# Moving the SBUF start addresses of weights, activations and gates in a fused attention and gated feed-forward kernel

## The chip, the cores and the metric

The kernel runs on one core of a Trainium2 chip. The metric is the device time of one execution in microseconds (us), the median of several runs. The text also speaks of the *span*: the time from the first to the last instruction of one profiled execution.

## The reference

Eight batches of eight attention heads: 512 local positions (which see 32 global keys and a band of local keys within 32 positions) and 32 global positions (which see all keys). The heads' outputs side by side form x, and a feed-forward block with a depthwise convolution as its gate follows.

```
s_g = scale * np.matmul(q_g, k_all.transpose(0, 1, 3, 2))
out_g = np.matmul(sm(s_g), v_all)
mask = np.abs(pos[:, None] - pos[None, :]) <= window          # window = 32
s_ll = np.where(mask, s_ll, -1000000000.0)
out_l = np.matmul(sm(np.concatenate([s_lg, s_ll], axis=-1)), np.concatenate([v_g, v_l], axis=2))
x = np.concatenate([out_g, out_l], axis=2)    # heads side by side: (8, 544, 512)
h = np.maximum(x @ w_in, 0.0)                 # (8, 544, 1024)
conv_out[:, s] = sum(conv_w[k] * h[:, s + k - 1] for k in range(3))
return (h * sigmoid(conv_out)) @ w_out        # (8, 544, 512)
```

## The kernel before

Everything lies with 128 rows in SBUF's 128 partitions. x, the gates g and both weight matrices are held as two float32r parts each, a high and a low one, and a product is the sum of three matmuls: high by high, high by low, low by high.

- **Attention** (lines 292 to 516): scores S (line 333) and G (line 354), maximum with mask (366), exponential (376), normalisation (390 or 397), 32x32 transposes (405), P·V (429). These are small matmuls that share the array in tiles of 32 or 64 rows.
- **x.** `XH` and `XL` (lines 447 and 455) write a batch's x, `[P, 2, NCT, SL]`: high and low part, four chunks of 512 columns of 2,048 bytes. The 32 global rows and the two rows beside them of all batches go to `xg` (line 271), `[P, 2, NCT, 8, 34]`, whose chunks are 272 columns, 1,088 bytes.
- **Up projection, `Z`** (line 533, matmul on 541): for each of 8 blocks of 128 hidden columns and each of 4 chunks three matmuls with a 128x128 block of `w_in` as weights. They come in runs of six (`Za`, `Zb`). A batch has 96 of 512 columns; the last unit, for the collected rows, has 96 of 272 columns that read `xg`.
- **Gate**: `RE` (ReLU into `hb`, one of two buffers that take turns from one pair of blocks to the next; line 554 on ScalarE), `C1` (317, GpSimd), `Ca` and `Cb` (568, VectorE), `TH` (575, ScalarE), `GG` (579, VectorE), `GH` and `GL` (278 and 281), which write g, `[P, 2, 2, SL]`.
- **Down projection, `O`** (line 591, matmul on 599): 4 blocks of output columns, 24 matmuls each, in runs of six (`Oa` to `Od`), weights from `w_out`. The last unit's have 278 columns. `OE` (line 278 again) and `ST` (611) store the result.
- **Weights** come as two 32-bit words per number in 8 pieces (`raw`, line 205, in the slots that g uses later), are taken apart on ScalarE, VectorE and GpSimd (`wt`, lines 141 to 163, in the slots of the gate's `t`), and for the first four pieces TensorE forms the low part in three matmuls per half (lines 257 to 259).

The order on every engine is fixed: `emit` (line 1038) plans all steps with a table of costs and due times and ties each instruction to the one ahead of it on its engine.

**SBUF addresses.** Tiles lie in the order in which pools are entered and tiles are made: `const` (line 89), `load`, `att`, `small` (92), `xp` (93, two slots of x), `moe` (94: `t` and `o`), `gp` (95: five slots of g). Every tile is rounded up to 32 bytes. `GM` (line 471) takes the negated maximum of a global softmax in a small tile of two columns, `GE` (482) takes the sum of the exponentials in another of one column, and `GN` and `GS` read that.

Of the kernel before, what the change touches and what calls it, by code (L numbers as in the profile page):

```python
# [11 lines left out]
F32 = mybir.dt.float32  # L12
# [6 lines left out]
P = 128  # L19
# [65 lines left out]
def attn_moe(ctx: ExitStack, tc: tile.TileContext, q_d, k_d, vw_d, qg_d, w_in_d, w_out_d, cw_d, out_d):  # L85
# [3 lines left out]
    const = ctx.enter_context(tc.tile_pool(name="const", bufs=1))  # L89
    load = ctx.enter_context(tc.tile_pool(name="load", bufs=2))  # L90
    att = ctx.enter_context(tc.tile_pool(name="att", bufs=2))
    small = ctx.enter_context(tc.tile_pool(name="small", bufs=4))
    xp = ctx.enter_context(tc.tile_pool(name="xp", bufs=SLOTS["x"]))
    moe = ctx.enter_context(tc.tile_pool(name="moe", bufs=2))
    gp = ctx.enter_context(tc.tile_pool(name="gp", bufs=SLOTS["g"]))
# [100 lines left out]
    def choice(key):  # L196
        return ENGS[phase[0]][key]

    w_in = [const.tile([P, NFT, NCT, P], F32R, name=f"w_in{i}") for i in range(2)]
    w_out = [const.tile([P, NCT, NFT, P], F32R, name=f"w_out{i}") for i in range(2)]  # L200
    raw = {}
# [269 lines left out]
    def GM(n):  # L471
        gr = groups[n]
        pg = gr["pg"] = pgs[n % 2]
        negm = gr["m"] = small.tile([P, 2], F32, name="gnegm", bufs=SLOTS["pg"])
        for i, (ps, sl) in enumerate(((gr["s0"], slice(SG, S)), (gr["s1"], slice(0, SG)))):
            nc.vector.tensor_scalar(  # L476
                out=pg[:, sl], in0=ps, scalar1=-SCALE, scalar2=None, op0=ALU.mult, op1=ALU.min,
                accum_out=negm[:, i : i + 1],
            )
        nc.vector.tensor_tensor(out=negm[:, 0:1], in0=negm[:, 0:1], in1=negm[:, 1:2], op=ALU.min)  # L480

    def GE(n):
        gr = groups[n]
        gr["r"] = small.tile([P, 1], F32, name="gsum", bufs=SLOTS["pg"])
        nc.scalar.activation(
            out=gr["pg"][:, 0:S], in_=gr["pg"][:, 0:S], func=AF.Exp, scale=-1.0, bias=gr["m"][:, 0:1], accum_out=gr["r"]
        )
# [120 lines left out]
    def ST(o):  # L608
# [5 lines left out]
        LQ=LQ, LK=LK, LV=LV, XC=XC, LG=LG, G=G, S=SC, M=MA, E=EX, NS=NS, NP=NP, DT=DT, P=PV,  # L614
        XH0=lambda n: XH(n, 0), XH1=lambda n: XH(n, 1), XL0=lambda n: XL(n, 0), XL1=lambda n: XL(n, 1),
        GM=GM, GE=GE, GN=GN, GX=GX, GS=GS, XG=XG,
        Za=lambda u: Z(u, 0), Zb=lambda u: Z(u, 1), RE=RE, C1=C1, Ca=lambda u: C2(u, 0), Cb=lambda u: C2(u, 2), TH=TH, GG=GG, GH=GH, GL=GL,
        Oa=lambda o: O(o, 0), Ob=lambda o: O(o, 1),
# [11 lines left out]
SLOTS = dict(  # L630
    ps=4, pa=2, x=2, hb=2, q=3, k0=1, k1=1, k2=1, k3=1, vf=2, qg=2, p0=2, p1=2, m=6, r=3, pg=2, go=2, t=2, o=2, g=5,
)
# [454 lines left out]
def program(arrays):  # L1087
    import concourse.bacc as bacc

    nc = bacc.Bacc("TRN2", target_bir_lowering=False, num_devices=1, dynamic_dma_scratch_size=1024)  # L1090
    args = [nc.dram_tensor(n, a.shape, mybir.dt.from_np(a.dtype), kind="ExternalInput").ap() for n, a in arrays.items()]
    args = [a.bitcast(U32) if a.dtype == mybir.dt.uint64 else a for a in args]
    B = arrays["q"].shape[0]
    out = nc.dram_tensor("out", (P, NCT * (B * (SL + GV) - 2)), F32, kind="ExternalOutput").ap()
    with tile.TileContext(nc, schedule_with_timeline_sim=True) as tc:
        attn_moe(tc, *args, out)
    return nc
# [19 lines left out]
```

## Time and profile before

| | |
|---|---|
| median of 3 runs | 543.51 us (543.3 to 543.71) |
| the profiled execution's own time | 543.3 us |
| its span | 541.4 us |
| TensorE matmul busy | 498.3 us (92%) of the span |
| VectorE, ScalarE, GpSimd busy | 420.5, 332.9, 102.9 us |
| matmuls of Z and O with 512 columns | 768 + 768 |
| matmuls of Z with 272 columns, of O with 278 | 96 + 96 |

PE is TensorE's matmul, PEld its weight load (which runs beside matmuls), DVE VectorE, ACT ScalarE, POOL GpSimd, SP the queue that issues DMAs. A matmul's duration in the rows includes its way through the array, so matmuls that follow each other overlap: their spacing is read from a run of several, or from the starts of two neighbours. An execution's time exceeds its span by 1.9 us here.

### The profile page before, as it was taken

What the parts mean: (1) busy time and instruction counts of PE and PEld (TensorE: products, weight loads), DVE (VectorE), ACT (ScalarE), POOL (GpSimd) and SP (SyncE); (2) the same over time, 40 slices, a digit from 0 to 9 for tenths busy, and PEclk for the clock granted to TensorE, in tenths of its full rate; (3) what the DMA queues carried; (4) which work ended last, traced back from release to release, by engine and by line L of the source; (5) the groups of instructions that cost most, each with busy time, mean ns of one, the idle gap of its engine ahead of it and who ended that gap; (6) DMA issues with size and microseconds to landing.
All of it is one profiled execution on the core that took longest, in us unless ns stands there. A gap on an engine that the chain in (4) does not pass through costs nothing.

```text
span 541.4 us, 16508 instructions
## 1 busy us (share of the span) xinstructions
PE 498.3 (92%) x6752; PEld 399.9 (74%) x6752; DVE 420.5 (78%) x1263; ACT 332.9 (61%) x1016; POOL 102.9 (19%) x153
## 2 busy tenths in 40 slices
PE   1945499989999999999999999999999999999997
PEld 0534378768788778788878877787878888888887
DVE  6988889999798878889788868987597884555451
ACT  3885969958658967983787239953379633233130
POOL 3474212442310111021011011111110211111110
PEclk9967689989999999999999999999999999999999
DMA  9986747341523231251324232410210000001101
GB/s 337 404 303 171 181 116 166 114 113 52 118 73 95 88 116 54 97 151 50 110 61 131 69 104 67 127 71 21 69 42 21 23 19 22 19 19 41 40 32 50
DMA packets 32668, 53.56 MB, mean 99 GB/s; under 512 B 2384, under 2 KB 20304, under 8 KB 31568
## 3 DMA queue, kind: packets, MB, share of 16 engines
q1 hardware_dynamic: 31440, 48.31, 26.8%
q0 software_dynamic: 1152, 4.19, 4.1%
q8 instruction: 53, 0.87, 0.7%
q14 instruction: 23, 0.19, 0.1%
HBM read 39.35 MB, written 8.96 MB: 89 GB/s over the span
## 4 chain that ended last, share of the span: by engine, by line
PE 88%; DVE 8%; ACT 2%; issue 1%; DMA 1%; SPq 0%; DVEq 0%
PE ps_o L599 36%; PE ps_h L541 35%; PE four L429 9%; PE four L333 5%; PE four L354 1%; ACT pt L376 1%; DVE pt L405 1%; DVE wt L154 1%; DVE t L568 1%; DVE pt L366 1%; DMA cwr<-cw 1%; PE psw L257 1%; DVE x L457 1%; DVE pg L476 1%; DVE wt L151 0%
## 5 line engine op out<-in xcount | busy, mean ns | idle before, releaser
L599 PE MATMUL ps_o<-g,w_out 128*128 128x512 f32 (+1 forms) x864 | 211.5, 385 | 0.0
L541 PE MATMUL ps_h<-x,w_in 128*128 128x512 f32 x768 | 202.3, 401 | 5.9 <-DVE x L457 4.1
L599 PEld LDWEIGHTS ps_o<-g,w_out 128*128 128x128 f32 x864 | 154.9, 188 | 34.9 <-issue 1.7
L541 PEld LDWEIGHTS ps_h<-x,w_in 128*128 128x128 f32 x768 | 143.1, 189 | 42.0 <-DVE x L457 4.8
L568 DVE SCALAR_TENSOR_TENSOR t<-hb,cw,t 128x512 f32<-128x512 f32 (+1 forms) x144 | 103.2, 736 | 34.6 <-POOL t L317 34.0
L317 POOL TENSOR_SCALAR t<-hb,cw 128x512 f32<-128x512 f32 (+1 forms) x72 | 53.7, 750 | 325.8 <-ACT hb L554 279.3
L376 ACT ACTIVATE pt<-pt,negm 128x128 f32<-128x128 f32 x256 | 99.2, 394 | 12.5 <-DVE negm L366 12.5
L554 ACT ACTIVATE hb<-ps_h 128x512 f32<-128x512 f32 (+1 forms) x72 | 41.4, 575 | 84.7 <-PE ps_h L541 84.4
L390 ACT ACTIVATE pt<-pt,sums 128x128 f32<-128x128 f32 x224 | 69.0, 396 | 0.9 <-DVE sums L383 0.9
L575 ACT ACTIVATE t<-t 128x1024 f32<-128x1024 f32 (+1 forms) x36 | 36.6, 1016 | 37.4 <-DVE t L568 37.4
L429 PE MATMUL four<-pt,vf 32*64 32x128 f32 (+3 forms) x2560 | 48.9, 294 | 10.6 <-DVE pt L405 3.8
L429 PEld LDWEIGHTS four<-pt,vf 32*64 32x64 f32 x2560 | 44.5, 139 | 17.3 <-issue 9.3
L366 DVE CUSTOM_DVE_ANT_0 pt<-four,mask 128x128 f32<-128x128 f32 x256 | 55.6, 285 | 2.1 <-PE four L333 2.1
L405 DVE STREAM_TRANSPOSE pt<-pt 128x608 f32<-128x608 f32 (+1 forms) x64 | 52.2, 851 | 1.6 <-ACT pt L390 1.6
L579 DVE SCALAR_TENSOR_TENSOR t<-t,hb 128x1024 f32<-128x1024 f32 (+1 forms) x36 | 42.3, 1174 | 13.1 <-ACT t L575 12.8
L376 ACT ACTIVATION_READ_ACCUMULATOR pt<-pt,negm 128x1 f32 x256 | 49.5, 193 | 0.0
L278 ACT CAST g<-t 128x1024 fp32r<-128x1024 f32 (+1 forms) x36 | 36.2, 1005 | 14.9 <-DVE t L579 10.6
L281 DVE TENSOR_TENSOR g<-t,g 128x1024 fp32r<-128x1024 f32 (+1 forms) x32 | 37.8, 1182 | 7.0 <-ACT g L278 6.7
L333 PE MATMUL four<-k,q 64*32 64x128 f32 x2048 | 36.0, 288 | 6.9 <-DVE pg L476 3.6
L333 PEld LDWEIGHTS four<-k,q 64*32 64x32 f32 x2048 | 31.0, 111 | 13.6 <-issue 4.8
L278 ACT CAST x<-four 128x384 fp32r<-128x384 f32 x64 | 19.4, 383 | 22.5 <-PE four L429 19.6
L278 DVE COPY o<-ps_o 128x512 f32<-128x512 f32 (+1 forms) x28 | 18.3, 653 | 16.2 <-PE ps_o L599 16.2
(70 smaller groups left out, 329.7 us busy)
## 6 DMA issues: line engine op xcount, KB each, us to landing
vf<-vw SPq DMA_DIRECT2D x16, 640.0 KB, 4.6
q<-q SPq DMA_DIRECT2D x32, 256.0 KB, 4.0
out<-o SPq DMA_DIRECT2D x32, 256.0 KB, 2.1
k<-k SPq DMA_DIRECT2D x24, 320.0 KB, 3.7
raw<-w_in SPq DMA_DIRECT2D x4, 1024.0 KB, 8.3
raw<-w_out SPq DMA_DIRECT2D x4, 1024.0 KB, 12.3
k<-k SPq DMA_DIRECT2D x8, 448.0 KB, 3.5
wt<-raw POOLq DMA_DIRECT2D x4, 512.0 KB, 5.2
```

Source lines behind the costliest of these rows:

```text
L278: nc.scalar.copy(out=out, in_=in_) if choice(key) == "a" else eng(key).tensor_copy(out=out, in_=in_)
L317: nc.gpsimd.tensor_scalar(out=out, in0=in_, scalar1=by, scalar2=0.0, op0=ALU.mult, op1=ALU.add)
L333: nc.tensor.matmul(heads[n + j]["s"][c * SG : (c + 1) * SG, r, :], lhsT=q[rows, c, r * SG : (r + 1) * SG], rhs=keys[rows, c, a : a + P], s ...
L366: nc.vector.tensor_tensor_reduce(out=out, in0=st["s"][:, r, :], in1=mask[:, v : v + 4].rearrange("p a c -> p (a c)"), op0=ALU.add, op1=ALU ...
L376: nc.scalar.activation(out=p, in_=p, func=AF.Exp, scale=-1.0, bias=st["m"][:, r : r + 1], accum_out=two["r"][:, n % 2, r : r + 1],)
L390: nc.scalar.activation(out=p, in_=p, func=AF.Copy, scale=by[:, r : r + 1])
L405: nc.vector.transpose(out=t, in_=t)
L429: nc.tensor.matmul(out, lhsT=vf[rows, j, s, :], rhs=pt, start=s == order[0], stop=s == order[-1])
L541: nc.tensor.matmul(hid[u]["z"], lhsT=w[:, ft, ct, :], rhs=x, start=ct + i == 0, stop=ct == NCT - 1 and i == 2)
L568: nc.vector.scalar_tensor_tensor(out=t, in0=rows_of(u, k)[:, u % 2], scalar=cw[:, 3 * ft + k : 3 * ft + k + 1], in1=t, op0=ALU.mult, op1=A ...
L579: nc.vector.scalar_tensor_tensor(out=t, in0=t, scalar=1.0, in1=rows_of(u, 1), op0=ALU.add, op1=ALU.mult)
L599: nc.tensor.matmul(ps, lhsT=w_out[w][:, mt, ft, :], rhs=g[:, k, ft % 2, :], start=ft + i == 0, stop=ft == NFT - 1 and i == 2,)
```

## The change

Two tiles that nothing reads or writes are put in, one of 96 bytes between the pools `small` and `xp`, one of 128 bytes ahead of `w_in`. The sum of the global softmax moves into a third column of the tile of the maximum, so that one small tile per slot is left instead of two.

```
+    gap = ctx.enter_context(tc.tile_pool(name="gap", bufs=1))
+    gap.tile([P, 24], F32, name="gap")
     xp = ctx.enter_context(tc.tile_pool(name="xp", bufs=SLOTS["x"]))
...
+    const.tile([P, 32], F32, name="gap")
     w_in = [const.tile([P, NFT, NCT, P], F32R, name=f"w_in{i}") for i in range(2)]
...
-        negm = gr["m"] = small.tile([P, 2], F32, name="gnegm", bufs=SLOTS["pg"])
+        negm = gr["m"] = small.tile([P, 3], F32, name="gnegm", bufs=SLOTS["pg"])
...
-        gr["r"] = small.tile([P, 1], F32, name="gsum", bufs=SLOTS["pg"])
+        gr["r"] = gr["m"][:, 2:3]
```

The start addresses in the two built programs (bytes within a partition; "rest" is the remainder by 256):

| tile | start before | rest | start after | rest |
|---|---|---|---|---|
| `plus`, `minus`, `pg`, `pt`, `mask`, `k`, `cw` | | | the same | the same |
| `w_in`, two parts | 41600, 57984 | 128 | 41728, 58112 | 0 |
| `w_out`, two parts | 74368, 90752 | 128 | 74496, 90880 | 0 |
| `xg` | 107136 | 128 | 107264 | 0 |
| `hb`, two slots | 115840, 119968 | 128, 160 | 115968, 120096 | 0, 32 |
| `qg`, `vf`, `q` | from 124096 | 192 | from 124224 | 64 |
| `x`, two slots | 142944, 159328 | 96 | 143104, 159488 | 0 |
| `t` and `wt`, two slots | 175712, 179808 | 96 | 175872, 179968 | 0 |
| `o`, two slots | 183904, 185952 | 96 | 184064, 186112 | 0 |
| `g` and `raw`, five slots | from 188000 | 96 | from 188160 | 0 |

Blocks of weights are 512 bytes apart and chunks of x and g 2,048, so every weight block, every chunk of x and every chunk of g has its tile's rest. Chunks of `xg` are 1,088 bytes apart, so theirs steps by 64. [...]

The order of instructions on all five engines is the same before and after, and so are the engines that each waits for; where a row named the one-column tile `gsum`, it now names `gnegm`.

## Rows read from the trace of the kernel before

**Rows 1.** The page: busy time, and the chain that ended last, by engine and line.
```profile
PE 498.3 (92%) x6752; PEld 399.9 (74%) x6752; DVE 420.5 (78%) x1263; ACT 332.9 (61%) x1016; POOL 102.9 (19%) x153
...
PE 88%; DVE 8%; ACT 2%; issue 1%; DMA 1%; SPq 0%; DVEq 0%
PE ps_o L599 36%; PE ps_h L541 35%; PE four L429 9%; PE four L333 5%; PE four L354 1%; ACT pt L376 1%; DVE pt L405 1%; DVE wt L154 1%; DVE t L568 1%; DVE pt L366 1%; DMA cwr<-cw 1%; PE psw L257 1%; DVE x L457 1%; DVE pg L476 1%; DVE wt L151 0%
```
**Rows 2.** Busy time by stretch: PE, PEld, DVE, ACT, POOL, PE's granted clock, DMA share, GB/s.
```profile
0.00:80.00 80.00, 45.73 (x1108) 31.71 (x1113) 66.74 (x255) 54.91 (x179) 32.04 (x64) 0.81 0.78 256
80.00:160.00 80.00, 77.33 (x1108) 61.75 (x1098) 73.31 (x189) 59.42 (x176) 25.21 (x24) 0.98 0.40 107
160.00:523.00 363.00, 360.22 (x4465) 292.18 (x4450) 275.05 (x810) 216.88 (x660) 45.16 (x64) 1.00 0.20 65
```
**Rows 3.** The chain in order of time, 448 to 523 us: start, us, what.
```profile
448.06 1.40 PE ps_h L541 x6
449.46 1.40 PE ps_o L599 x6
450.87 1.40 PE ps_h L541 x6
...
490.06 0.75 PE ps_h L541 x6
490.81 1.40 PE ps_o L599 x6
492.21 0.76 PE ps_h L541 x6
```
**Rows 4.** Lines 541 and 599: matmuls by width, duration ns min/median/max, first and last start.
```profile
L541 PE MATMUL ps_h<-x,w_in x690: 387/396/628, 103.6 to 488.3; 128*128 128x512 f32 x173
L541 PE MATMUL ps_h<-xg,w_in x1: 290/290/290, 489.9 to 489.9; 128*128 128x272 f32 x1
...
L541 PE MATMUL ps_h<-xg,w_in x96: 282/288/294, 489.9 to 522.7; 128*128 128x272 f32 x96
...
L599 PE MATMUL ps_o<-g,w_out x81: 289/289/296, 526.8 to 537.0; 128*128 128x278 f32 x81
```
**Rows 5.** Timeline of PE, 13 to 15 and 72 to 75 us: start, us, what.
```profile
13.84 0.63 PE L259 MATMUL psw<-w_in,minus 128*128 128x512 f32 x1
14.27 1.91 PE L257 MATMUL psw<-wt,plus 128*128 128x512 f32 x2
...
73.45 0.40 PE L259 MATMUL psw<-w_in,minus 128*128 128x512 f32 x1
73.68 1.02 PE L257 MATMUL psw<-wt,plus 128*128 128x512 f32 x2
```
**Rows 6.** Timelines of ACT, POOL and DVE, 455 to 475 us: start, us, what.
```profile
455.16 0.60 ACT L554 ACTIVATE hb<-ps_h 128x512 f32<-128x512 f32 x1 [4.07 <-PE ps_h L541]
460.76 0.60 ACT L554 ACTIVATE hb<-ps_h 128x512 f32<-128x512 f32 x1 [1.20 <-PE ps_h L541]
466.36 0.60 ACT L554 ACTIVATE hb<-ps_h 128x512 f32<-128x512 f32 x1 [4.07 <-PE ps_h L541]
471.96 0.60 ACT L554 ACTIVATE hb<-ps_h 128x512 f32<-128x512 f32 x1 [1.49 <-PE ps_h L541]
...
455.85 0.69 POOL L317 TENSOR_SCALAR t<-hb,cw 128x512 f32<-128x512 f32 x1 [4.90 <-ACT hb L554]
467.05 0.69 POOL L317 TENSOR_SCALAR t<-hb,cw 128x512 f32<-128x512 f32 x1 [4.91 <-ACT hb L554]
...
459.60 1.22 DVE L579 SCALAR_TENSOR_TENSOR t<-t,hb 128x1024 f32<-128x1024 f32 x1 [1.48 <-ACT t L575]
470.50 1.23 DVE L579 SCALAR_TENSOR_TENSOR t<-t,hb 128x1024 f32<-128x1024 f32 x1 [1.19 <-ACT t L575]
```
**Rows 7.** The page: DMA issues, count, KB each, us to landing.
```profile
raw<-w_in SPq DMA_DIRECT2D x4, 1024.0 KB, 8.3
wt<-raw POOLq DMA_DIRECT2D x4, 512.0 KB, 5.2
```
**Rows 8.** Who waited for whom: us in total, times, longest.
```profile
PE psw L257 <- DVE wt L154: 10.5, 1, 10.5
...
PE four L333 <- DMA q<-q: 1.0, 1, 1.0
```
**Rows 9.** Groups of instructions of the global softmax: count, busy us, mean ns, idle before.
```profile
L485 ACT ACTIVATE pg<-pg,gnegm 128x544 f32<-128x544 f32 x16 | 12.0, 751 | 3.4 <-DVE gnegm L480 3.3
...
L492 DVE TENSOR_SCALAR gsum<-gsum 128x1 f32<-128x1 f32 x16 | 2.2, 138 | 2.0 <-ACT pg L485 2.0
```

## The prediction

> **What bounds the kernel now.** I read the page first. PE is busy 498.3 of 541.4 us and holds 88% of the chain that ended last, 71% on lines 541 and 599 alone [rows 1]. Next the stretches: from 160 to 523 us PE is busy 360.2 of 363.0 us at the full granted clock, 2.4 GHz (1.00); only in the first 80 us is it idle for long, with the clock at 0.81 on average [rows 2]. So behind the start the time is the number of matmuls times their spacing.
>
> The chain in order of time gives the spacing: six matmuls of 512 columns in 1.40 us, 233 ns each, on line 541 as on line 599; six of 272 columns in 0.75 to 0.76 us, 126 ns each [rows 3]. Durations by width give the 278-column ones: 289 against 396 ns, 107 ns less, so 233 - 107 = 126 ns [rows 4]. Columns alone would need 512 / 2.4 = 213, 272 / 2.4 = 113 and 278 / 2.4 = 116 ns. So there is an **excess** of 20, 12.5 and 10.5 ns, and this is what an address could touch. At half the clock there is none: one matmul of line 259 begins at 13.84 and its neighbour at 14.27 us, 0.43 us later, where 512 / 1.2 is 0.427 [rows 5].
>
> **The change part by part.** The sum is made against the profiled execution, 543.3 us, its span of 541.4 and 1.9 around it; the median of the runs shown stands 0.2 above.
>
> *Order and waits.* Both stay as they are on all engines, and the two gap tiles issue nothing. 0 us. No step is moved past any queue.
>
> *The merged column.* Sixteen exponentials (751 ns each) put their sum 8 bytes behind the bias that they read, instead of into another tile; two tiny VectorE steps for each then work there [rows 9]. Same count, same widths, same waits. The tile now lives until the last reader of the sum, but that reader also reads the softmax's big tile, which the next maximum of that slot overwrites and so waits for already. 0 us. Were each of the 16 late by the 2.0 us that the whole group of line 492 now waits, it would still be hidden for the last seven batches, since PE has other batches' projections to work on there.
>
> *ScalarE, VectorE, GpSimd.* Their operands move from rest 96 to rest 0. The trace has this experiment in it: the two `hb` buffers lie at rests 128 and 160, so one begins at a multiple of 64 bytes and the other 32 bytes past one. Four ReLUs in a row, at most two on one buffer, take 0.60 us each; C1 takes 0.69 on either, and the VectorE product behind the tanh 1.22 and 1.23 [rows 6]. So no engine tells 0 from 32. I take 0. The bounds are the rows' last digit, 0.01 us in either direction, on engines that PE does not wait for between 160 and 523 us; lost cover would show as idle time on PE, which is 2.8 us there [rows 2].
>
> *DMAs.* Raw weights land at rest 0 rather than 96, the accumulating DMAs and the stores read from rest 0. One megabyte takes 8.3 us to land, half a megabyte SBUF to SBUF 5.2 [rows 7]. In all of PE's waits a DMA is the last releaser once, for q, 1.0 us, and the longest wait is for VectorE's bits, 10.5 us [rows 8]. Bounds: between nothing and that 1.0 us, both ways. I take 0.
>
> *TensorE's operands, the one large term.* 768 + 768 matmuls of 512 columns begin their moving operand at rest 0 instead of 96 and load weights from rest 0 instead of 128; 96 of 278 columns likewise; 96 of 272 columns step by 64 bytes as before. Each ns per matmul on 1,536 is 1.5 us. No row has both operands at rest 0, so I bound it. Upper gain: the whole excess of 20 ns goes. Upper loss: the 272-column matmuls, whose starts step through the phases against weights that do not, take 282 to 294 ns around a median of 288 [rows 4], so a start can cost 6 ns. The nearest row is line 259 at full clock: its moving operand is the high part of `w_in`, at rest 128, and its weights, `minus`, lie at rest 128 too, both multiples of 64 and of 128. Its neighbour begins 73.68 - 73.45 = 0.23 us later [rows 5], as much as x at rest 96 needs [rows 3]. From 32-byte to 128-byte starts nothing was gained within the 10 ns of that view; and the 272-column matmuls, all starting at multiples of 64, have an excess of 12.5 ns where 278 columns from rest 96 have 10.5. So I take 0 ns per matmul.
>
> Sum: 543.3 + 0 = **543.3 us**; with 0.7 ns either way per matmul, which these rows can't exclude, 542.2 to 544.4.
>
> **The rivals.**
> 1. *One edge less.* The excess could be paid at each aligned 256-byte piece that a moving operand touches. From rest 96, 2,048 bytes touch nine pieces: 20 / 9 = 2.2 ns each. 1,112 bytes (278 columns) touch five: 10.5 / 5 = 2.1. 1,088 bytes touch five from any of their starts: 2.5. That the three agree speaks for it, and line 259, nine pieces from rest 128, fits as well. From rest 0 the wide ones touch eight, the narrow ones still five: 2.2 ns x 1,536 = 3.4 us less, 539.9 us. Against it: an excess of 0.038 ns per column without any edge gives the same three numbers. By pieces of 128 bytes the gain would be 20 / 17 x 1,536 = 1.8 us, by 64 bytes 20 / 33 x 1,536 = 0.9 us, which is nearly the forecast. [...]
> 2. *The whole excess goes.* If only rest 0 on both sides lets the moving operand stream freely, 20 ns x 1,536 + 10.5 x 96 = 31.7 us go, 511.6 us. Against it: a quarter of the 272-column matmuls start at rest 0 already, and even their shortest, 282 ns, is only 6 below the median, where 12.5 would have to go [rows 4]. What is left is that their weights lay at rest 128. [...]
> 3. *Slower: the two streams now keep step.* While a matmul streams, the next weights load. Until now x and g began 32 bytes before the weights' place within 512 bytes; now both begin at 256 within 512, the same place. If equal places collide, each matmul pays. The trace has one such pair: the first 272-column matmul began at rest 128 of 512 with weights at 128 of 512 and took 290 ns [rows 4], 2 above the median of its width; against 278 columns from rest 96, less six columns at 107 / 234 = 0.46 ns (286.3), it is 3.7. So 2 x 1,632 = 3.3 to 3.7 x 1,632 = 6.0 us more: 546.6 to 549.3 us. It decides from 0.7 ns per matmul on. Against it: a spread of 12 ns in that group may come from the weights just loaded rather than from the start.
> 4. *The gaps are not where they should be.* A tile that nothing uses could be dropped. The addresses of the built program speak against it; the time would be 543.3.
>
> **How the numbers follow.** A measurement can tell about 0.2% from no change, 1.1 us. The forecast has a chance of 0.46 and the fourth rival 0.02: both within 0.2%, 0.48. One edge less has 0.27 and the whole excess 0.06: faster, 0.33. Streams in step have 0.19: slower. The likeliest case's own range is 542.2 to 544.4. The range goes down to 539.6, which takes in one edge less, and up to 547.3, which takes in the lower price of the third rival; outside are the second rival, 0.06, and the dearer half of the third, 0.08.
>
> **What would show it.** Right: six matmuls on the chain still take 1.40 us, ReLU 0.60 and C1 0.69 us, PE's busy time stays near 498 us, and the idle time ahead of it in the first 80 us keeps its releasers. One edge less would show as 1.386 us for six, with the 272- and 278-column medians (288 and 289 ns) unmoved. Streams in step would show as 1.41 to 1.42 us for six and medians of 398 and more. I am wrong if the spacing of the wide matmuls moves by more than 0.7 ns, or if the time moves and the spacing does not: then the cause lies in the first 80 us, in a different granted clock there or in an earlier or later first batch.

## The result, and the profile after

The changed kernel takes **535.29 us** (median of four runs, 535.23 to 535.73) where the kernel before takes 543.4 (543.04 to 543.71) beside it: a ratio of 0.9853 with a 95% interval of 0.9836 to 0.987, 8.1 us less. The forecast of 543.3 was wrong, and the time lies below its range of 539.6 to 547.3. The profiled execution took 535.33 us, its span 533.4. Lines stand two or three further down in the code now: 154 is 156, 541 is 544, 599 is 602, 554 is 557.

First the page of the changed kernel, its parts as in [rows 1]:

```profile
PE 491.7 (92%) x6752; PEld 401.3 (75%) x6752; DVE 420.3 (79%) x1263; ACT 332.8 (62%) x1016; POOL 105.5 (20%) x153
...
PE 84%; DVE 8%; ACT 5%; issue 1%; DMA 1%; SPq 0%; DVEq 0%
```

Its busy time by stretch, in the columns of [rows 2]:

```profile
0.00:80.00 80.00, 47.32 (x1071) 33.02 (x1076) 66.94 (x255) 54.36 (x177) 32.20 (x64) 0.77 0.78 256
80.00:160.00 80.00, 76.72 (x1171) 62.58 (x1161) 73.58 (x190) 60.25 (x180) 25.20 (x24) 0.98 0.39 107
160.00:515.00 355.00, 352.56 (x4440) 291.33 (x4424) 274.26 (x810) 216.47 (x659) 47.64 (x64) 1.00 0.21 66
```

Busy time has moved by 0.2 us at most on DVE and ACT and risen by 2.6 us on POOL, whose spans are rough, and TensorE has lost 6.6 us of busy time with the same 6,752 matmuls. The stretch behind 160 us, at a granted clock of 1.00 and with as little idle time as before (2.4 and 2.8 us) [rows 2], is 8 us shorter. So what changed is the matmul itself. The chain that ended last, in order of time (start, us, what), shows it:

```profile
448.53 1.36 PE ps_o L602 x6
449.89 1.36 PE ps_h L544 x6
...
482.53 0.76 PE ps_h L544 x6
483.29 1.39 PE ps_o L602 x6
485.42 1.36 PE ps_o L602 x6
```

Six matmuls of 512 columns take 1.36 us where they took 1.40 [rows 3], 226.7 ns each instead of 233.3; six of 272 columns still take 0.76. Behind runs of 272 columns, wide runs take 1.39 and 1.36 by turns. Behind an attention step the starts settle to 226.7 ns at once in some places and only after up to ten matmuls in others. Over all neighbouring wide matmuls at a granted clock of 1.00 the mean spacing went from 233.2 to 227.5 ns. 5.7 x 1,536 = 8.8 us, against 8.0 off the span.

The duration of one, which goes on past the start of the next, says the same (line 544: ns min/median/max):

```profile
L544 PE MATMUL ps_h<-x,w_in x690: 387/389/628, 103.7 to 480.8; 128*128 128x512 f32 x173
```

The median is 389, where [rows 4] has 396. The remaining 0.8 us were lost in the first 160 us. The matmuls come in the same order in both traces, so their starts can be set side by side. The 2,251st of 6,752 begins at 160.4 us, 0.4 us earlier than before; 276 wide ones lie ahead of it, and at 5.7 ns each they would give 1.6 us. From there to the last the gain is 7.6 us more, against 1,260 x 5.7 = 7.2. In the first part TensorE still waits for other engines: between 80 and 160 us its idle time rose from 2.7 to 3.3 us [rows 2]. The granted clock of the first 80 us was lower too, 0.77 against 0.81 [rows 2], but e4_x128 below has 0.81 there, and its 2,251st matmul is no further ahead (0.3 us).

### The profile page after: what moved, and what is told of

Same layout as the page of the kernel before. It is cut to its first block, busy times and chain, and to the rows that moved or that the text cites. A ratio compares the mean times of both kernels' runs of the same rounds, so it can differ in the third digit from the quotient of the medians.

```text
span 533.4 us, 16508 instructions
## 1 busy us (share of the span) xinstructions
PE 491.7 (92%) x6752; PEld 401.3 (75%) x6752; DVE 420.3 (79%) x1263; ACT 332.8 (62%) x1016; POOL 105.5 (20%) x153
## 4 chain that ended last, share of the span: by engine, by line
PE 84%; DVE 8%; ACT 5%; issue 1%; DMA 1%; SPq 0%; DVEq 0%
PE ps_o L602 35%; PE ps_h L544 33%; PE four L432 8%; PE four L336 6%; ACT pt L379 2%; DVE pt L369 1%; PE psw L260 1%; DVE pt L408 1%; PE four L357 1%; DVE wt L156 1%; DVE t L571 1%; DMA cwr<-cw 1%; ACT pt L393 1%; DVE x L460 1%; DVE pg L479 1%
## 5 line engine op out<-in xcount | busy, mean ns | idle before, releaser
L602 PE MATMUL ps_o<-g,w_out 128*128 128x512 f32 (+1 forms) x864 | 207.0, 380 | 0.0
L544 PE MATMUL ps_h<-x,w_in 128*128 128x512 f32 x768 | 197.8, 396 | 6.6 <-DVE x L460 4.4
L320 POOL TENSOR_SCALAR t<-hb,cw 128x512 f32<-128x512 f32 (+1 forms) x72 | 56.3, 787 | 316.6 <-ACT hb L557 284.5
L336 PE MATMUL four<-k,q 64*32 64x128 f32 x2048 | 37.9, 299 | 6.4 <-DVE pg L479 3.6
L336 PEld LDWEIGHTS four<-k,q 64*32 64x32 f32 x2048 | 32.8, 116 | 13.1 <-issue 4.4
```

The costliest lines, as they stand in the source:

```text
L320: nc.gpsimd.tensor_scalar(out=out, in0=in_, scalar1=by, scalar2=0.0, op0=ALU.mult, op1=ALU.add)
L336: nc.tensor.matmul(heads[n + j]["s"][c * SG : (c + 1) * SG, r, :], lhsT=q[rows, c, r * SG : (r + 1) * SG], rhs=keys[rows, c, a : a + P], s ...
L544: nc.tensor.matmul(hid[u]["z"], lhsT=w[:, ft, ct, :], rhs=x, start=ct + i == 0, stop=ct == NCT - 1 and i == 2)
L602: nc.tensor.matmul(ps, lhsT=w_out[w][:, mt, ft, :], rhs=g[:, k, ft % 2, :], start=ft + i == 0, stop=ft == NFT - 1 and i == 2,)
```

## The experiments

**Theories.** A: the excess depends on where the moving operand begins. B: it depends on how the moving operand and the weights that load beside it lie to each other. C: it depends on where the weights begin. A fourth possibility is that the merged column did it. A', in two of the expectations, is that both must begin at multiples of 256. Below, *distance* is the moving operand's start less the weights', modulo 256 bytes. The kernel before has 96 - 128, that is 224; the changed one 0. Spacings called settled are read from the starts of neighbours behind the first matmuls of a group. The small kernels (m1 to m5) were run once each, at a mean granted clock of 1.00. Ratios are to the kernel before in the same session, where its medians were 543.53 to 544.87 us.

**m1_scan.** A small kernel that times nothing but wide matmuls of the same kind, the moving operand begun at `a` to `p` (0 to 480 bytes in steps of 32) and the weights at `a` to `d` (0, 128, 256, 384), 36 for each pair.

```
+    for dw in range(4):
+        for dx in range(16):
...
+                        nc.tensor.matmul(
+                            ps, lhsT=block(4 * w + ct, 32 * dw), rhs=chunk(4 * x + ct, 8 * dx),
```

> The attention and the feed-forward block are left out; the output is zeros. TensorE runs 64 groups of 36 matmuls of 512 columns of float32r, in the order and strides of a run of the up projection. Group x?w?: the moving operand begins at 0, 32, 64 ... 480 (a to p) within 512 bytes, the weights at 0, 128, 256, 384 (a to d). Theory A (only the moving operand's start counts): spacing 226.7 ns for xa and xi whatever the weights, 233.3 for the others. Theory B (the stream of the matmul and the load of the next weights get in each other's way, so the difference of the two starts counts): the same spacing along the diagonals, xa-wa like xe-wb, xi-wc, xm-wd, and 233.3 on others, the pair of the kernel before, xd-wb, among them. Theory C (only the weights' start counts): 226.7 for wa and wc with every x, 233.3 for wb and wd.

The chain, one row for each pair (start, us, names: `xdwb` is x at 96 and weights at 128, the kernel before):

```profile
37.16 8.41 PE xdwa L96 x36
...
79.19 8.19 PE xiwa L96 x36
...
171.29 8.40 PE xdwb L96 x36
179.69 8.19 PE xewb L96 x36
187.87 8.40 PE xfwb L96 x36
196.27 8.25 PE xgwb L96 x36
...
212.94 8.40 PE xiwb L96 x36
```

8.40 / 36 = 233.3 ns. `xewb` has both at 128 and settles at 226.7; `xiwa` has 256 against 0, the same; `xiwb` has 256 against 128 and gets nothing, although x is as aligned as in `xiwa`. All 64 pairs follow the distance alone: settled spacings of 226.7 ns at 0, 228.9 at 64, 234.4 at 160 and 233.3 to 233.5 at 32, 96, 128, 192 and 224. B holds; neither start matters by itself.

**e1_weights, e2_x.** In the whole kernel, one side each. e1 makes the weight tiles ahead of `cwr`, so that they begin at rest 0 and x stays at 96 (distance 96). e2 puts a gap of 160 bytes ahead of x alone, so that x, t, o and g begin at rest 0 and the weights stay at 128 (distance 128).

```
e1:
+    w_in = [const.tile([P, NFT, NCT, P], F32R, name=f"w_in{i}") for i in range(2)]
+    w_out = [const.tile([P, NCT, NFT, P], F32R, name=f"w_out{i}") for i in range(2)]
     cwr = const.tile([P, 3 * NFT, wpe], WT, name="cwr")
e2:
+    gap = ctx.enter_context(tc.tile_pool(name="gap", bufs=1))
+    gap.tile([P, 40], F32, name="gap")
     xp = ctx.enter_context(tc.tile_pool(name="xp", bufs=SLOTS["x"]))
```

> Only the weights move, to rest 0 by 256 (41216, by making their tiles ahead of the three small tiles of conv_w); x, t, o, g, xg and hb keep their addresses. Theory A: no change, 543.4 us, six matmuls in 1.40 us. Theory B: faster than before if the distance of 416 bytes (or 160 by 256) between x and weights is a good one, between 535 and 543. Theory C: all of the change, 535.3 us, six in 1.36 us.

> Only x, t, o and g move, to rest 0 by 256 as in the change (gap of 160 bytes, no merged tile); the weights stay at rest 128. Theory A: all of the change, 535.3 us, six matmuls in 1.36 us. Theory B: between 535 and 543 by the new distance of 128 bytes. Theory C: no change, 543.4 us.

e1: 544.91 us, ratio 1.0004 (0.9993 to 1.0015), six matmuls in 1.40 us. e2: 543.96, ratio 0.9988 (0.9976 to 1.0), six in 1.39 to 1.40. A row from the chain of each, e1 first:

```profile
450.26 1.40 PE ps_h L541 x6
...
449.62 1.39 PE ps_o L601 x6
```

Half of the alignment is worth nothing clear of noise, on either side: A and C fall. B has no gain here either, since m1_scan has 233.3 to 233.5 ns for the distances 96 and 128.

**e3_merge.** The merged column alone, with a gap of 64 bytes that keeps the large tiles where they were.

```
+    gap.tile([P, 16], F32, name="gap")
...
-        gr["r"] = small.tile([P, 1], F32, name="gsum", bufs=SLOTS["pg"])
+        gr["r"] = gr["m"][:, 2:3]
```

> Only the merged column of the global softmax, with a gap of 64 bytes behind it, so that weights, x and all large tiles keep the addresses of the kernel before. Every theory on addresses: no change, 543 to 545 us with the kernel before beside it, ratio 1.000. If the merged tile itself gains or costs something, it shows here.

544.68 us, ratio 1.0012 (0.9995 to 1.003), six in 1.40 us: the merged column changes nothing that can be told from noise. The chain:

```profile
446.75 1.40 PE ps_h L543 x6
```

**e4_x128.** One gap of 32 bytes ahead of x and nothing else: x, t, o and g at rest 128, the weights left at 128. Distance 0, and no operand of a wide matmul at a multiple of 256.

```
+    gap.tile([P, 8], F32, name="gap")
```

> One gap of 32 bytes ahead of x, and nothing else: weights and xg stay at rest 128, x, t, o and g move from rest 96 to rest 128. No operand of the wide matmuls begins at a multiple of 256, but the distance of the two is 0, as after the change. Theory B (distance): all of the change, ratio 0.985, six matmuls in 1.36 us. Theory A' (both must begin at multiples of 256): no change, ratio 1.000, 1.40 us.

535.63 us, ratio 0.9852 (0.9826 to 0.9879): all of the gain. The chain from 446 us on, and the first 80 us in the columns of [rows 2]:

```profile
446.13 1.36 PE ps_o L601 x6
447.49 1.36 PE ps_h L543 x6
...
0.00:80.00 80.00, 45.49 (x1086) 31.46 (x1091) 67.09 (x255) 54.44 (x177) 32.26 (x64) 0.81 0.79 256
```

**e6_x192.** The same gap with `[P, 24]`: x at 192, distance 64, where m1_scan has 228.9 ns.

> One gap of 96 bytes ahead of x, and nothing else: weights at rest 128, x, t, o and g at rest 192, so the distance is 64, for which m1_scan showed 228.9 ns. Theory B with that table: two thirds of the change's gain, (233.3 - 228.9) / (233.3 - 226.7) = 0.67 of 8.0 us, ratio 0.990, six matmuls in 1.37 to 1.38 us. Theory A' (both at multiples of 256): ratio 1.000.

538.61 us, ratio 0.9909 (0.9892 to 0.9925): some six tenths of the gain, where m1_scan has (233.3 - 228.9) / 6.7, two thirds of it. The chain:

```profile
448.14 1.37 PE ps_o L601 x6
449.51 1.37 PE ps_h L543 x6
```

**m2_sizes.** Small kernel: widths, narrower weights and bfloat16, at distance 0 (`ma`) and at the places of the kernel before (`mb`), 48 each. In bfloat16 the same column offsets are half as many bytes, 48 and 64 in `mb`, a distance of 240.

```
+    for s, dx, dw in (("a", 0, 0), ("b", 24, 32)):
+        for n, cols in ((512, "n"), (384, "o"), (272, "p"), (256, "q"), (192, "r"), (128, "s")):
+            group("m" + s + cols, n, P, dx, dw)
+        for m, rows in ((64, "t"), (32, "u")):
+            group("m" + s + rows, SL, m, dx, dw)
...
+        group("m" + s + "bf", SL, P, dx, dw, xb, wb)
```

> The attention and the feed-forward block are left out; the output is zeros. Groups of 48 matmuls at both operands on a multiple of 512 bytes (ma...) and at the places of the kernel before (mb...): widths 512, 384, 272, 256, 192, 128 (n to s), weights of 64 and 32 columns (t, u), one weight block again and again (same), bfloat16 (bf). If the excess over columns / 2.4 GHz is paid to the load of the next weights (theory B), it falls with narrow weights, to a half at 64 columns (3 and 7 ns less in ma and mb than at 128), and is gone in bfloat16, whose two streams read half the bytes. If it belongs to the moving operand alone (A), 64 and 32 columns of weights leave 226.7 and 233.3 as they are, and the excess goes with the width: 13 to 20 ns at 512, half of that at 256.

Settled spacings, distance 0 / before: 512 columns 226.7 / 233.3, 384 columns 173.3 / 173.3, 272 columns 125.6 / 126.7, 256 columns 120 / 118.3, 192 and 128 columns 111.7 both. Weights of 64 columns give 230 / 231.7 and of 32 columns 231.7 / 240. In bfloat16 both places give 215.8. One weight block loaded again and again, in the 4-byte type, leaves 226.7 / 233.3. Rows of the chain (`mat` and `mbu` have weights of 64 and 32 columns, `bf` is bfloat16, `mbn` the kernel before):

```profile
54.02 11.05 PE mat L99 x48
...
87.09 10.38 PE mabf L99 x48
97.46 11.19 PE mbn L99 x48
...
150.53 11.49 PE mbu L99 x48
...
173.21 10.38 PE mbbf L99 x48
```

At distance 0 the steps from 256 to 384 and from 384 to 512 columns take 53.3 and 53.4 ns, 2.4 columns per ns, and 512 columns at that rate are 213.3 ns. Two readings that the expectation had fall: A's, that the excess goes with the columns (384 columns have 13.3 ns over their 160 at either distance), and B's, that it shrinks to a half when fewer weights load beside a matmul. At 256 columns distance 0 is even the slower place. In bfloat16 only 2.5 ns over 213.3 are left.

**m3_fine.** The scan again in steps of 4 bytes, and two groups whose weights alternate between rests 0 and 128: the moving start matches its own weights (`own`), or those that load while it streams (`next`).

```
+    for hi in range(8):
+        for lo in range(8):
+            group("x" + "abcdefgh"[hi] + "abcdefgh"[lo], [(8 * hi + lo, 0)] * 36)
+    group("own", [(32 * (k % 2), 32 * (k % 2)) for k in range(48)])
+    group("next", [(32 * ((k + 1) % 2), 32 * (k % 2)) for k in range(48)])
```

> The attention and the feed-forward block are left out; the output is zeros. As m1_scan, with the weights always at 0 and the moving operand 4 bytes further in each of 64 groups (x and two letters: 32-byte step a to h, 4-byte step a to h in it). By theory B as m1_scan left it (the distance by 256 decides) groups aa, ba, ca ... repeat 226.7, 233.4, 228.9, 233.3, 233.3, 234.4, 233.3, 233.3 ns; if the pieces that collide are of 32 bytes or more, starts in between lie near one of their neighbours, and none is below 226.7; if they are smaller, some start is. Groups own and next: weights alternate between 0 and 128; in own each moving operand begins where its own weights began, in next where the weights began that load while it streams. If the load beside a matmul is what it collides with, next gives 226.7 and own 233.3; if it is its own weights, the other way round.

Starts at multiples of 32 repeat m1_scan; those between give 228.3 to 240 ns, and none is below 226.7. They do not lie near their neighbours: 4 bytes behind distance 0 it is 237.7 ns. The two groups, 48 each:

```profile
550.26 11.35 PE own L93 x48
561.61 11.04 PE next L93 x48
```

They settle at 236.7 and 230.0 ns. So matching the weights that load beside the matmul helps, and matching its own does not; 226.7 isn't reached with alternating weights, and why not is open.

**m4_load.** Does the excess come from the reading of the two operands? All weight columns are read from one address (`wzero`), or from every second (`wtwo`), or all moving columns from one (`xzero`), at distances 0 (`a`), 224 (`b`) and 64 (`c`).

```
+            if wstep != 1:
+                lhsT = bass.AP(lhsT.tensor, lhsT.offset, [lhsT.ap[0], [wstep, P]])
+            if xstep != 1:
+                rhs = bass.AP(rhs.tensor, rhs.offset, [rhs.ap[0], [xstep, SL]])
```

> The attention and the feed-forward block are left out; the output is zeros. Groups of 48 matmuls of 512 columns at three distances of moving operand less weights by 256 bytes: 0 (a), 224 as in the kernel before (b), 64 (c). plain: as m1_scan. wzero: the weights' columns are all read from one address. wtwo: from every second one. xzero: the moving columns are all read from one address. both: both from one address. If the load of the next weights collides with the moving operand by address (theory B), wzero no longer has three different spacings, and wtwo moves them too; with xzero nothing steps through the addresses any more and the excess over 213.3 ns falls for all three. If the excess came from the moving operand's own way through its addresses (A), wzero and wtwo would leave 226.7, 233.3, 228.9 as they are, and only xzero would change them.

```profile
23.04 11.10 PE wzeroa L97 x48
...
45.34 10.36 PE xzeroa L97 x48
...
66.06 11.19 PE plainb L97 x48
77.25 11.12 PE wzerob L97 x48
...
99.50 10.36 PE xzerob L97 x48
...
120.22 11.00 PE plainc L97 x48
131.22 11.10 PE wzeroc L97 x48
```

With the moving columns from one address all of the excess but 2.5 ns is gone (10.36 / 48 = 215.8 ns) at every distance. With the weights from one address the three distances become alike, 231.1 to 231.7 ns. So the excess needs a moving operand that walks through addresses, and the weights' addresses set how much of it is paid. A collision of the two reads would do that, but it is argued and not shown: no run leaves the weight load out, and what the two would collide in, no run shows.

**m5_patterns.** If it is a walk in step, another order of walking should change it: weights from every fourth and eighth address, moving columns backwards (`r`), in two turns over the two halves (`h`: 0, 256, 1, 257, ...), in four (`q`), and others.

```
+    W = dict(l=None, b=[[4, P]], c=[[8, P]])
+    X = dict(l=None, r=[[-1, SL]], h=[[1, 256], [256, 2]], e=[[1, 2], [2, 256]], f=[[1, 4], [4, 128]], q=[[1, 128], [128, 4]], s=[[1, 16], [16, 32]], t=[[1, 64], [64, 8]])
```

> The attention and the feed-forward block are left out; the output is zeros. Groups of 36 matmuls of 512 columns at distance 0 (a) and 224 (b). First pair of letters, the weights: l in a row, b and c every fourth and every eighth address. Second pair, the moving columns: l in a row, r backwards, h, q, t, s, f, e in 2, 4, 8, 32, 128, 256 turns over 256, 128, 64, 16, 4, 2 runs (h: 0, 256, 1, 257 ...). reva... : backwards, at distances 32 to 224. The question is whether an order of addresses comes below 226.7 ns towards the 215.8 that m4_load showed with moving columns from one address. If the collisions are between pieces of some size, orders that stay in a piece as briefly as possible (h, q) are slower than 233, and backwards columns have a best distance of their own, near 226.7. If stepping as such costs the rest, none is below 226.7.

The chain, 36 each; `a` is distance 0, `b` the places before:

```profile
37.76 8.40 PE wlxra L99 x36
46.16 7.77 PE wlxha L99 x36
...
86.78 10.18 PE wlxqa L99 x36
...
130.14 8.39 PE wlxlb L99 x36
...
164.31 7.77 PE wlxhb L99 x36
...
324.44 8.50 PE wbxh L99 x36
```

Weights from every fourth or eighth address cost more (235.0 and 244.4 ns at distance 0). Backwards loses the good distance (233.3 at every one). Four turns are worse (283.3 and 273.3 ns), and the orders in more turns take 433 to 493 ns. Two turns, against what was expected, settle at 215.8 ns at either distance, 2.5 over the 213.3 of m2_sizes. They do so with weights in a row; with every fourth address (`wbxh`) it is 236.7 ns.

**e7_turns, e8_turns_after.** This goes into the kernel before (e7) and into the changed one (e8): Z and O read their moving operand in two turns, and RE and OE, which copy the result out of PSUM, put the columns back in order as they read.

```
+    def in_turn(ap):
+        return ap.rearrange("p (j k) -> p k j", j=2)
...
-                    ps, lhsT=w_out[w][:, mt, ft, :], rhs=g[:, k, ft % 2, :], start=ft + i == 0,
+                    ps, lhsT=w_out[w][:, mt, ft, :], rhs=in_turn(g[:, k, ft % 2, :]), start=ft + i == 0,
...
-        cp("OE", t, ops[o])
+        cp("OE", t.rearrange("p (j k) -> p j k", j=2), ops[o].rearrange("p (k j) -> p j k", j=2))
```

> The kernel before with all its addresses, but the projections' moving columns are read in two turns (0, 256, 1, 257 ...), which m5_patterns showed at 215.8 ns for either distance; ReLU and the result's copy read PSUM in the matching order. Theory B (collisions of streams that step through SBUF side by side): spacing 215.8 in place of 233.3 ns, 17.5 x 1,536 = 26.9 us off PE, 516.5 us if ScalarE and VectorE keep up, ratio 0.950; some of it comes back as waits, since VectorE is busy 275 of 363 us behind the start: 0.95 to 0.965. If the pattern only helps in the small program, ratio 1.000.

> The changed kernel with the same reading in two turns. By m5_patterns the distance no longer matters then: the same time as e7_turns within 0.3%, and the change is worth nothing on top of it. If the address still counts in two turns, 5 to 8 us less than e7_turns.

Both take 518.02 us: ratio 0.9523 (0.9506 to 0.954) for e7 and 0.9532 (0.951 to 0.9553) for e8. That is some 17 us below the changed kernel, and the addresses make no difference any more. Of e7, the page, and below it the stretches from 80 us in the columns of [rows 2]:

```profile
PE 470.9 (91%) x6752; PEld 400.0 (77%) x6752; DVE 421.0 (82%) x1263; ACT 331.3 (64%) x1016; POOL 108.7 (21%) x153
...
PE 77%; DVE 13%; ACT 7%; issue 2%; DMA 1%; SPq 0%; DVEq 0%
...
80.00:160.00 80.00, 75.87 (x1233) 64.17 (x1219) 75.46 (x196) 61.56 (x181) 27.40 (x25) 0.98 0.40 108
160.00:500.00 340.00, 336.67 (x4342) 291.72 (x4341) 273.15 (x805) 213.90 (x658) 48.94 (x65) 1.00 0.22 69
```

And the chain of e7, 446 to 469 us:

```profile
446.31 1.29 PE ps_o L605 x6
447.61 1.29 PE ps_h L544 x6
...
468.33 0.69 PE ps_h L544 x6
```

Six take 1.29 us. The copies read PSUM every 8 bytes for it, at no cost: ReLU 576 ns on average against 575 before, the copies on VectorE 649 against 653. 233.3 - 215.8 = 17.5 ns x 1,536 = 26.9 us, and the span lost 25.2. What is missing was again lost ahead of 160 us: the 2,251st matmul is 2.2 us ahead, where 276 x 17.5 ns are 4.8, and TensorE is idle for 4.1 us between 80 and 160 us, 2.7 before [rows 2]. VectorE and ScalarE hold 20% of the chain where they held 10% [rows 1], and that share lies in this first part; behind 160 us TensorE is idle for 3.3 of 340 us, hardly more than the 2.8 of 363 before.

## Why the prediction was wrong

*Right:* that the time behind the start is matmuls times spacing, at full clock (1.00 from 160 us on [rows 2]); that the excess over columns at 2.4 per ns is what an address can touch (all of it but 2.5 ns, m4_load); and each term set to nothing but one. Order and waits: the same work, engine by engine. The merged column: e3_merge, ratio 1.0012, and its sixteen exponentials still take 748 ns [rows 9]. ScalarE, in the timeline of the kernel after (start, us, what):

```profile
448.63 0.60 ACT L557 ACTIVATE hb<-ps_h 128x512 f32<-128x512 f32 x1 [3.90 <-PE ps_h L544]
454.07 0.60 ACT L557 ACTIVATE hb<-ps_h 128x512 f32<-128x512 f32 x1 [1.03 <-PE ps_h L544]
```

And GpSimd, in the same columns:

```profile
443.88 0.70 POOL L320 TENSOR_SCALAR t<-hb,cw 128x512 f32<-128x512 f32 x1 [4.74 <-ACT hb L557]
```

0.60 and 0.70 us stand against 0.60 and 0.69 [rows 6]. The conclusion held, though its reading was loose: ReLU writes and C1 reads from the second column of `hb` on, so in [rows 6] no operand in `hb` begins at a multiple of 64 bytes. It is the row after, whose C1 writes `t` at rest 0, that shows the aligned case. The DMAs land as before too; from the page after, in the columns of [rows 7]:

```profile
raw<-w_in SPq DMA_DIRECT2D x4, 1024.0 KB, 8.2
...
wt<-raw POOLq DMA_DIRECT2D x4, 512.0 KB, 5.3
```

The longest wait of TensorE is still that for the weights' bits, 10.4 us (who waited for whom, as in [rows 8]):

```profile
PE psw L260 <- DVE wt L156: 10.4, 1, 10.4
```

The rate of 2.4 columns per ns (the prediction's 2.4 GHz) stood in none of its rows, but the traces show it. In the kernel before, four matmuls of 512 columns on line 541 begin 427, 426 and 427 ns apart from 67.44 us on, where the view has a granted clock of 0.50: 1.2 columns per ns, without an excess. At 1.00 the steps in width of m2_sizes give 2.4. At 13.84 us, which the prediction calls half the clock [rows 5], the next start is 427 ns away too, but the view has a granted clock of 1.00 there: that row alone does not show it.

*The step that failed* is the term "TensorE's operands", taken as 0 ns per matmul within 0.7. It measured -5.7 ns on average and -6.7 once settled. Its nearest row was line 259 with both operands at rest 128, read as "0.23 us, as much as x at rest 96 needs" [rows 5]. Both operands at the same rest is distance 0: the row was an instance of the very case that the change makes, and not, as the text had it, a case of aligned starts without a gain. It could not show that, for two reasons: its digit is 10 ns, where the effect is 6.7 and the range claimed was 0.7; and it is one matmul between others, while a wide run can need up to ten to settle. By the starts themselves, the four places of the trace before, behind 16 us, where line 259 is followed at once have 225 to 235 ns, all at a granted clock of 1.00. The second support, the 272-column matmuls, is a width at which the two places of m2_sizes differ by 1.1 ns, and the 278-column ones beside them, read from durations as 126 ns, follow each other in 127.2 by their starts, and in 126.7 after. So "no row has both operands at rest 0" was right by the letter and missed that the rest was not the quantity.

*The rivals.* "One edge less" fell: 226.7 and not 231.1 ns, and rest 0 without a matching partner gave nothing (e2_x). The excess per column set against it gives 10.3 ns and not 12.5 at 272 columns, so it never fitted all three widths either. "Streams in step" had the right quantity, the place of one stream against the other, and the wrong sign: equal places are the good case, and the two ns between 290 and 288 [rows 4] on which its price rested were no sign of a loss. "The whole excess goes" was wrong of this change, which takes 6.7 of 20 ns. Elsewhere all of it but 2.5 ns does go: bfloat16 has 215.8 ns for 512 columns at both places (m2_sizes), and so has the 4-byte type once its columns come in two turns (m5_patterns); the 17.5 x 1,536 = 26.9 us that follow from this are within two of the 25.2 that e7_turns took off the span. "The gaps are not where they should be" was rightly set near zero.

*Open:* what the two reads share (no run shows a size of it), why narrower weights do not make it less, why 384 columns pay the same at 0 and at 224, and why two turns avoid it. That distance 0 is the good case is shown; why it is, is not.

## What to carry to other kernels

Where matmuls of 4-byte operands follow each other, 512 columns wide as here, divide a long run on the chain by its count and compare with its columns at 2.4 per ns (m2_sizes, granted clock 1.00); if some per cent are over, as the 233.3 ns here are over 213.3, look at the distance of the two operands' starts modulo 256 bytes before anything else, and then at the order in which the moving columns are read. A bound from "the nearest row" is only as good as that row's digit: an effect of 7 ns on 1,536 matmuls is 10 us, and a single pair of rows in steps of 10 ns can neither show nor exclude it, where six or thirty-six in a row can. An edit that aligns everything may work through one relation alone; one gap of 32 bytes, ahead of x and the tiles behind it, did all of it here. At other widths measure first: at 384 columns the two places were alike, and at 256 distance 0 lost 1.7 ns.

## What the runs showed that I had not expected

- The spacing of 512-column matmuls in the 4-byte type ranges from 226.7 to 240 ns with the start addresses alone, and at multiples of 32 bytes it follows the distance between the two, not either's alignment.
- Reading the moving columns in two turns over the halves (8-byte steps in PSUM behind it) takes the excess away but for 2.5 ns: 215.8 ns, and 4.8% of this kernel's time.
- In the 4-byte type, matmuls of 128 columns follow each other no faster than those of 192: 111.7 ns for both, with 128x128 weights loading beside them.
